# Buffers, queues and engines around the scores of a streamed recurrent attention kernel

## The chip, the cores and the metric

The kernel runs on one core of one Trainium2 chip. The core has a matrix engine (TensorE, PE in the profile, with its weight loads as PEld), a vector engine (VectorE, DVE), a scalar engine (ScalarE, ACT), GpSimd (POOL) and SyncE (SP), and 16 transfer engines that carry the DMAs of all queues. The metric is the device time of one launch in microseconds, the median of several runs. Each engine works through its own list of instructions in the order in which the kernel wrote them; semaphores hold an instruction back until what it needs is done.

## What is computed

Two blocks share a normalised input and are added to it. Block A is attention over segments of 32 rows that carry 8 rows of memory along; block B is a feed-forward block on the two rows that a router scores highest. Cut to what matters:

```python
x = A_x                                # 2048 x 1024, bf16
xn = layernorm(x)
# A: 64 segments in sequence, H = 32 heads of E = 128, M = 8 memory rows
for s in range(64):
    h = concat([mem, xn[32*s : 32*s+32]])          # 40 rows
    q, k, v = h @ Wq, h @ Wk, h @ Wv               # 1024 -> 32 x 128 each
    p = softmax(mask(q @ k.T * 128**-0.5))         # 40 x 40 for each head
    o = (p @ v) @ Wo                               # 4096 -> 1024
    mem, out[32*s : 32*s+32] = o[:8], o[8:]
# B: top 2 rows of xn @ w_r
y = (silu(xs @ w_gate) * (xs @ w_up)) @ w_down * sigmoid(r)
return x + out + xn + scatter(y)
```

The next segment's first 8 rows are this segment's result, so the segments run one after the other, each through all four weight matrices of 1024 x 4096.

## The kernel before

The weights of block A take 64 granules of 128 x 2048 bf16 (512 KB each): 48 for q, k and v, 16 for the output. 42 stay in SBUF (`wres`), 22 are fetched anew in every segment, evenly spread over the 64, into six slots (`wstream`, tile `g`). SyncE issues these fetches (L248): as soon as the matmuls of a granule have been written down, `used(g)` issues the fetch of the granule six places later into the same slot.

A prologue normalises x, writes its transposes to DRAM, computes block B's rows and folds them into the residual `zT_d`. Then come 64 segments, s = 4G + j. Each runs six phases, `PHASES`: q, k for heads 0 to 15 (half 0), q, k for half 1, then v for both halves. A phase is eight steps kc over the contraction. A step is four matmuls side by side, `PSm[32*jq...] += ST[:, kc] @ granule` (L502), where `ST` holds 24 rows of the segment and the 8 memory rows. After the phases come 16 steps w of the output projection into `WO` (L543), and the result goes through `mem_to_st` into the next segment's `ST` (L266, L267).

The 8 rows of a segment that don't fit into these 32 are called the left rows. They don't depend on the memory, so those of four segments are done together: at j = 1 and j = 2 the q and the k of the next group of four (phases with a second accumulator `PSl`, L506), at j = 0 the v of this group (phases 4 and 5), and at j = 3 their output projection (`WL`). Left q and k go through a transpose (`transposes_left`, L414) to DRAM, `qkl_d`, and come back for each segment and half as the tile `QKL` (`load_qkl`, L355).

Work of other kinds is hung into the phases by `hook(p, kc, fn)`, which runs fn after the matmuls of step kc of phase p:

- the transposes of q or k of a phase at step 1 of the next (`transposes`, into PSUM tile `PTq`, which VectorE copies to `QT` or `KT`), those of left rows at step 2;
- `fetch_z` at (1, 4): loads the residual `ZT` on ScalarE's queue, and has GpSimd copy its left rows to `ZL` and set them to zero (L394, L395);
- `scores(0)` at (2, 5) and `scores(1)` at (4, 5): GpSimd copies the left k from `QKL` behind the 32 others in `KT` (L428), TensorE makes the scores in PSUM (L432 to L437), VectorE and ScalarE the softmax (L442 to L461), and then the next `QKL` is loaded into the one buffer (L357, on ScalarE's queue): after half 0 that of half 1 of the same segment, after half 1 that of half 0 of the next;
- `attend(half, ph)`: two at (5, 2) and (5, 5), two between the steps of the projection. They need `VM[half]`, the v of that half, and `VL`. ScalarE copies the main rows of the result to `OT`, VectorE the left ones to `OTL` (L483, L485).

At the end of phases 4 and 5 the accumulator of v is copied to `VM`, the left columns 0 to 255 by ScalarE, the others by VectorE (L524, L525; L527 and L528 for `VL`). At the end of a segment ScalarE issues four stores of the result (L572) and at j = 3 four more of the left rows (L584).

All DMAs of SyncE and ScalarE take their semaphores in turn from one set of eight (DMAHW0 to DMAHW7 in the lists below), in the order in which the program wrote them down. A DMA that takes a semaphore waits until the one that had it eight places earlier has landed, and its queue waits with it.

PSUM has eight banks: two for `PSm` and `WO` (`psA`), one for `PSl` and `WL` (`psL`), two for transposes (`psT`), one for the scores, two for attend (`psO`).

Of the kernel before, what the change touches and what calls it, by code (L numbers as in the profile page):

```python
# [8 lines left out]
BF16 = mybir.dt.bfloat16  # L9
# [16 lines left out]
def kernel(  # L26
# [63 lines left out]
    psL = ctx.enter_context(tc.tile_pool(name="psL", bufs=1, space=PSUM))  # L90
    psT = ctx.enter_context(tc.tile_pool(name="psT", bufs=2, space=PSUM))
# [78 lines left out]
    def ln_c(t):  # L170

        TS[t] = []
        for src, what in ((XN[t], "x"), (xt(t), "z")):
            PTx = psT.tile([P, KC, 4, SEG], BF16, tag="t", name="PTx")
# [179 lines left out]
    def load_qkl(s, half):  # L354

        t = one.tile([P, 2, P], BF16, tag="qkl", name="QKL")
# [11 lines left out]
    QKL = None  # L368

    for s in range(NSEG):  # L370
# [14 lines left out]
        QT, KT, PTs, OT, nxt = {}, {}, {}, {}, {"qkl": QKL}  # L385
# [5 lines left out]
        def fetch_z():  # L391
            Zt = nxt["z"] = one.tile([P, KC, SEG], BF16, tag="zt", name="ZT")
            nc.scalar.dma_start(out=Zt[:, :, :], in_=zT_d[s])
            nc.gpsimd.tensor_copy(out=ZL[:, :, j, :], in_=Zt[:, :, XM:SEG])  # L394
# [30 lines left out]
        def scores(half):  # L425
            QKL = load_qkl(0, half) if s == 0 else nxt.pop("qkl")
# [14 lines left out]
            NM = two.tile([P, 8], F32, tag="nm", name="NM")  # L441
# [3 lines left out]
            DN = two.tile([P, 8], F32, tag="dn", name="DN")  # L445
# [17 lines left out]
            if s > 0 or half == 1:  # L463
                s1, half1 = (s, 1) if half == 0 else (s + 1, 0)
                if s1 < NSEG:
                    nxt["qkl"] = load_qkl(s1, half1)

        def attend(half, ph):
# [4 lines left out]
            for il in range(4):  # L473
                for jl in range(2):
# [10 lines left out]
            nc.vector.tensor_copy(out=OTL[:, h0:h0 + 8, j, :].rearrange("p (a i) r -> p a i r", a=2),  # L485
                                  in_=ov[:, :, :, SEG:NK])

        hook(1, 4, fetch_z)
        hook(2, 3, fetch_st)
        hook(2, 5, lambda: scores(0))  # L490
        hook(4, 5, lambda: scores(1))
        hook(5, 2, lambda: attend(0, 0))
        hook(5, 5, lambda: attend(0, 1))

        for p, (mat, half) in enumerate(PHASES):
# [16 lines left out]
            if mat < 2:  # L512
# [3 lines left out]
                if PSl is not None:  # L516
                    XBl = two.tile([P, 512], BF16, tag="xb", name="XBl")
                    nc.vector.tensor_copy(out=XBl[:, :], in_=PSl[:, :])  # L518
                    hooks.setdefault((p + 1, 2), []).insert(
                        0, lambda m=mat, h=half, b=XBl, g=left[mat]: transposes_left(m, h, b, g))  # L520
            else:
                c0 = half * 512
                VM[half] = one.tile([P, 512], BF16, tag="vm", name="VM")
                nc.scalar.copy(out=VM[half][:, 0:256], in_=PSm[:, 0:256])  # L524
                nc.vector.tensor_copy(out=VM[half][:, 256:512], in_=PSm[:, 256:512])  # L525
                if PSl is not None:
                    nc.scalar.copy(out=VL[:, c0:c0 + 256], in_=PSl[:, 0:256])  # L527
                    nc.vector.tensor_copy(out=VL[:, c0 + 256:c0 + 512], in_=PSl[:, 256:512])  # L528
# [42 lines left out]
        for g in range(4):  # L571
            nc.scalar.dma_start(out=out2[s * SEG:s * SEG + XM, 256 * g:256 * (g + 1)], in_=OB[32 * g:32 * g + XM, :])  # L572
# [6 lines left out]
        if j == 3:  # L579
            OL = one.tile([P, 256], BF16, tag="pm", name="OL")  # L580
            nc.scalar.copy(out=OL[:, :], in_=WL[:, 0:256])
            o4 = out2[4 * G * SEG:4 * (G + 1) * SEG, :].rearrange("(s r) d -> s r d", s=4)
            for g in range(4):
                nc.scalar.dma_start(out=o4[:, XM:SEG, 256 * g:256 * (g + 1)], in_=OL[32 * g:32 * (g + 1), :])  # L584
        if s + 1 < NSEG:
            ST, QKL = nxt["st"], nxt["qkl"]

# [34 lines left out]
```

## Time and profile before

| | |
|---|---|
| median of 3 runs | 2657.51 us (2650.09 to 2669.58) |
| the profiled execution | 2657.51 us, span 2655.6 us |
| mean granted TensorE clock | 0.862 |
| busy: PE, PEld, DVE, ACT, POOL | 1887.9, 981.6, 721.6, 465.0, 111.1 us |
| moved by DMA | 831.71 MB, mean 313 GB/s |
| of it the granules' queue (SyncE's) | 795.98 MB in 292148 packets |
| ScalarE's queue | 30.46 MB in 76352 packets |
| first segment, with block B ahead of it | 105.0 to 239.7 us |
| segments 1 to 62 | 239.7 to 2610.5 us |
| last segment and the end | 2610.5 to 2655.6 us |

In the profile a line like `POOL KT L428 <- DMA QKL<-qkl_d` names the engine, the tile that it writes and the line, and behind the arrow what ended its idle time. In lists of waits the numbers are the total in microseconds, how often, and the longest. An engine with a q behind its name (SPq, ACTq) is its sequencer, which issues the DMAs. The DMA share of a stretch is the mean busy share of the 16 transfer engines, counted from packets.

### The profile page before, as it was taken

Reading aid. Unit: us, or ns where it says so; the run is one execution under the profiler, and the core shown is the slowest. Engines: PE = TensorE matmul, PEld = TensorE weight load, DVE = VectorE, ACT = ScalarE, POOL = GpSimd, SP = SyncE. Lnnn points to the kernel's source line nnn. Section 1 sums busy time; section 2 is a strip of 40 time slices with the busy share of each in tenths; the row PEclk is TensorE's granted clock in tenths of the full one; section 3 lists DMA queues with packets and bytes.
Section 4 is the critical chain, followed back from the end, with each engine's and each line's share of the span. In section 5 each row is a group of like instructions: output and inputs, shape, how many; then the busy total and the mean of one; then the engine's idle time right before and its main releaser. Section 6 shows DMA issues by size and latency. Waiting matters only on the chain.

```text
span 2655.6 us, 82564 instructions
## 1 busy us (share of the span) xinstructions
PE 1887.9 (71%) x36873; PEld 981.6 (37%) x36873; DVE 721.6 (27%) x2021; ACT 465.0 (18%) x1017; POOL 111.1 (4%) x371
## 2 busy tenths in 40 slices
PE   4357777677777767776777777777777767777676
PEld 3223343334334333333434333333434333343333
DVE  5202223222222322222222322223232222223222
ACT  4201111111111111111111111111111111111111
POOL 4100000000000000000000000000000000000000
PEclk8578889988898889888988898788888888879888
DMA  9986989989898889989898988989899898989987
GB/s 350 325 316 214 346 299 330 322 301 330 297 333 306 311 308 317 327 301 336 311 327 308 326 307 314 324 297 328 306 321 323 309 321 291 343 280 336 327 289 273
DMA packets 368856, 831.71 MB, mean 313 GB/s; under 512 B 69458, under 2 KB 122738, under 8 KB 368500
## 3 DMA queue, kind: packets, MB, share of 16 engines
q1 hardware_dynamic: 292148, 795.98, 84.8%
q10 hardware_dynamic: 76352, 30.46, 4.2%
q8 instruction: 288, 4.72, 0.7%
q14 instruction: 68, 0.56, 0.1%
HBM read 804.28 MB, written 22.02 MB: 311 GB/s over the span
## 4 chain that ended last, share of the span: by engine, by line
DMA 47%; PE 26%; DVE 11%; issue 10%; ACT 2%; ACTq 1%; POOL 1%; SPq 1%; POOLq 0%; DVEq 0%
DMA QKL<-qkl_d 12%; DMA g<-in_A_Wk_dram 11%; PE PSm L502 9%; DMA g<-in_A_Wq_dram 9%; PE WO L543 7%; DMA out_dram<-OB 3%; DMA ZT<-zT_d 3%; DVE SPS L443 2%; DVE NM L442 2%; PE OP L478 2%; PE PSl L506 2%; DVE DN L446 1%; PE WL L543 1%; ACT SPS L444 1%; DMA xT_d<-Tx 1%
## 5 line engine op out<-in xcount | busy, mean ns | idle before, releaser
L502 PE MATMUL PSm<-wres,ST 128*32 128x512 bf16 x8192 | 813.1, 438 | 22.3 <-DVE ST L267 13.6
L502 PE MATMUL PSm<-g,ST 128*32 128x512 bf16 x4096 | 459.1, 433 | 153.9 <-DMA g<-in_A_Wq_dram 94.6
L502 PEld LDWEIGHTS <-ST 128*32 128x32 bf16 x12288 | 333.7, 103 | 583.8 <-issue 290.7
L506 PE MATMUL PSl<-wres,STL 128*32 128x512 bf16 x2048 | 226.5, 428 | 52.8 <-DVE VL L528 47.9
L514 ACT CAST XB<-PSm 128x512 bf16<-128x512 f32 x256 | 150.3, 587 | 632.6 <-PE PSm L502 457.0
L543 PE MATMUL WO<-wres,OT 128*32 128x256 bf16 x5120 | 238.7, 289 | 3.7 <-issue 3.7
L543 PEld LDWEIGHTS <-OT 128*32 128x32 bf16 x8192 | 220.2, 104 | 31.0 <-issue 10.1
L432 PE MATMUL SPS<-KT,QT 128*32 128x40 bf16 x2048 | 51.2, 188 | 191.2 <-POOL KT L428 191.2
L442 DVE TENSOR_REDUCE NM<-SPS 128x8 f32<-128x320 f32 x128 | 63.0, 492 | 451.0 <-PE SPS L437 451.0
L478 PE MATMUL OP<-PT,VM 32*128 32x40 bf16 x2048 | 102.3, 186 | 107.0 <-DVE VM L525 73.2
L543 PE MATMUL WO<-g,OT 128*32 128x256 bf16 x3072 | 171.8, 301 | 2.2 <-issue 1.5
L444 ACT ACTIVATE SPS<-SPS 128x320 f32<-128x320 f32 x128 | 54.1, 423 | 674.9 <-DVE SPS L443 558.2
L483 ACT CAST OT<-OP 128x256 bf16<-128x256 f32 x256 | 95.5, 373 | 430.2 <-PE OP L480 430.2
L404 PE MATMUL PTq<-IDENT,XB 128*128 128x128 bf16 x1024 | 110.7, 236 | 77.6 <-ACT XB L514 75.2
L485 DVE CAST OTL<-OP 128x64 bf16<-128x64 f32 x256 | 57.6, 225 | 353.0 <-ACT OT L483 353.0
L478 PEld LDWEIGHTS <-VM 32*128 32x128 bf16 x2048 | 70.2, 95 | 224.3 <-issue 83.7
L506 PEld LDWEIGHTS <-STL 128*32 128x32 bf16 x3072 | 92.4, 104 | 139.8 <-issue 89.6
L404 PEld LDWEIGHTS <-XB 128*128 128x128 bf16 x1024 | 63.2, 103 | 212.4 <-ACT XB L514 195.3
L412 DVE COPY KT<-PTq 128x512 bf16<-128x512 bf16 x128 | 54.4, 425 | 317.9 <-PE PTq L404 284.9
L409 DVE COPY QT<-PTq 128x512 bf16<-128x512 bf16 x128 | 52.4, 409 | 262.8 <-PE PTq L404 262.8
L434 PEld LDWEIGHTS <-QKL 128*8 128x8 bf16 x2048 | 38.4, 87 | 219.9 <-issue 112.7
L506 PE MATMUL PSl<-g,STL 128*32 128x512 bf16 x1024 | 109.7, 412 | 7.0 <-DVE XBl L518 7.0
(100 smaller groups left out, 1573.6 us busy)
## 6 DMA issues: line engine op xcount, KB each, us to landing
g<-in_A_Wq_dram SPq DMA_DIRECT2D x384, 512.0 KB
g<-in_A_Wo_dram SPq DMA_DIRECT2D x384, 512.0 KB
g<-in_A_Wk_dram SPq DMA_DIRECT2D x320, 512.0 KB
g<-in_A_Wv_dram SPq DMA_DIRECT2D x320, 512.0 KB
qkl_d<-QS ACTq DMA_DIRECT2D x64, 128.0 KB
QKL<-qkl_d ACTq DMA_DIRECT2D x128, 64.0 KB
g<-in_B_w_gate_dram SPq DMA_DIRECT2D x16, 448.0 KB
g<-in_B_w_up_dram SPq DMA_DIRECT2D x16, 448.0 KB
```

The costliest lines, as they stand in the source:

```text
L404: nc.tensor.transpose(out=PTq[:, il, :, :].rearrange("p j r -> p (j r)"), in_=XB[:, il * P:(il + 1) * P], identity=IDENT[:, :])
L412: nc.vector.tensor_copy(out=KT[half][:, :, 0:32], in_=pv)
L442: nc.vector.tensor_reduce(out=NM[:, :], in_=S8, axis=AX.X, op=ALU.max, negate=True)
L443: nc.vector.tensor_tensor(out=S8, in0=S8, in1=NM[:, :].unsqueeze(2).to_broadcast([P, 8, NK]), op=ALU.add)
L444: nc.scalar.activation(out=S8, in_=S8, func=ACTF.Exp, scale=SCALE)
L478: nc.tensor.matmul(o, lhsT=VM[half][q0:q0 + 32, il * P:(il + 1) * P], rhs=PTm[q0:q0 + 32, il, 0:NK], start=True, stop=False, tile_position ...
L483: nc.scalar.copy(out=OT[half][:, 2 * ph:2 * ph + 2, :, :], in_=ov[:, :, :, 0:SEG])
L485: nc.vector.tensor_copy(out=OTL[:, h0:h0 + 8, j, :].rearrange("p (a i) r -> p a i r", a=2), in_=ov[:, :, :, SEG:NK])
L502: nc.tensor.matmul(PSm[32 * jq:32 * jq + 32, :], lhsT=ST[:, kc, :], rhs=Gv[:, 512 * jq:512 * (jq + 1)], start=(kc == 0), stop=(kc == KC - ...
L506: nc.tensor.matmul(PSl[32 * jq:32 * jq + 32, :], lhsT=STL[:, kc, :], rhs=Gv[:, 512 * jq:512 * (jq + 1)], start=(kc == 0), stop=(kc == KC - 1),
L514: nc.scalar.copy(out=XB[:, :], in_=PSm[:, :])
L543: nc.tensor.matmul(PS[32 * g:32 * g + 32, 0:256], lhsT=lhs(h), rhs=Gv[:, D * hs + 256 * g:D * hs + 256 * (g + 1)], start=False, stop=(last ...
```

## The change

Five edits, with no change to the arithmetic:

- `QKL` gets two buffers. After scores(half) of segment s the left q and k of (s + 1, half) are loaded. Segment 0 loads its own at its scores, as before, and both of segment 1 at its end.
- `fetch_z` keeps only the load. GpSimd's copy to `ZL` and the memset become `split_z`, at (4, 6), behind scores(1).
- `VM` and `VL` are copied whole by ScalarE; so is `OTL` for half 0.
- `psL` gets two banks, `psT` one. In the prologue the transposes of z use `psO`. The transposes of left rows move from step 2 to step 3.
- The stores of a segment's result are put into a list `todo` and issued by SyncE in the next segment, at (0, 2), those of left rows at (0, 5). `NM` and `DN` go to one buffer each.

```diff
-    psL = ctx.enter_context(tc.tile_pool(name="psL", bufs=1, space=PSUM))
-    psT = ctx.enter_context(tc.tile_pool(name="psT", bufs=2, space=PSUM))
+    psL = ctx.enter_context(tc.tile_pool(name="psL", bufs=2, space=PSUM))
+    psT = ctx.enter_context(tc.tile_pool(name="psT", bufs=1, space=PSUM))
...
-        t = one.tile([P, 2, P], BF16, tag="qkl", name="QKL")
+        t = two.tile([P, 2, P], BF16, tag="qkl", name="QKL")
...
             nc.scalar.dma_start(out=Zt[:, :, :], in_=zT_d[s])
+
+        def split_z():
+            Zt = nxt["z"]
             nc.gpsimd.tensor_copy(out=ZL[:, :, j, :], in_=Zt[:, :, XM:SEG])
             nc.gpsimd.memset(Zt[:, :, XM:SEG], 0.0)
...
-            QKL = load_qkl(0, half) if s == 0 else nxt.pop("qkl")
+            QKL = load_qkl(0, half) if s == 0 else QKLs.pop(0)
...
-            if s > 0 or half == 1:
-                s1, half1 = (s, 1) if half == 0 else (s + 1, 0)
-                if s1 < NSEG:
-                    nxt["qkl"] = load_qkl(s1, half1)
+            if s == 0 and half == 1:
+                QKLs.append(load_qkl(1, 0))
+                QKLs.append(load_qkl(1, 1))
+            elif 0 < s < NSEG - 1:
+                QKLs.append(load_qkl(s + 1, half))
...
-            nc.vector.tensor_copy(out=OTL[:, h0:h0 + 8, j, :].rearrange("p (a i) r -> p a i r", a=2),
-                                  in_=ov[:, :, :, SEG:NK])
-
+            (nc.scalar.copy if half == 0 else nc.vector.tensor_copy)(
+                out=OTL[:, h0:h0 + 8, j, :].rearrange("p (a i) r -> p a i r", a=2), in_=ov[:, :, :, SEG:NK])
+
+        for n, fn in enumerate(todo):
+            hook(0, 2 + 3 * n, fn)
...
+        hook(4, 6, split_z)
...
-                    hooks.setdefault((p + 1, 2), []).insert(
+                    hooks.setdefault((p + 1, 3), []).insert(
...
-                nc.scalar.copy(out=VM[half][:, 0:256], in_=PSm[:, 0:256])
-                nc.vector.tensor_copy(out=VM[half][:, 256:512], in_=PSm[:, 256:512])
+                nc.scalar.copy(out=VM[half][:, :], in_=PSm[:, :])
                 if PSl is not None:
-                    nc.scalar.copy(out=VL[:, c0:c0 + 256], in_=PSl[:, 0:256])
-                    nc.vector.tensor_copy(out=VL[:, c0 + 256:c0 + 512], in_=PSl[:, 256:512])
+                    nc.scalar.copy(out=VL[:, c0:c0 + 512], in_=PSl[:, :])
...
-        for g in range(4):
-            nc.scalar.dma_start(out=out2[s * SEG:s * SEG + XM, 256 * g:256 * (g + 1)], in_=OB[32 * g:32 * g + XM, :])
+        def store(OB=OB, s=s):
+            for g in range(4):
+                nc.sync.dma_start(out=out2[s * SEG:s * SEG + XM, 256 * g:256 * (g + 1)],
+                                  in_=OB[32 * g:32 * g + XM, :])
+
+        todo = [store]
...
+                    nc.sync.dma_start(out=o4[:, XM:SEG, 256 * g:256 * (g + 1)], in_=OL[32 * g:32 * (g + 1), :])
+            todo.append(store_left)
```

What this makes of the order is seen at three places. First ScalarE's list where a group of four segments ends and the next begins (j = 3 to j = 0), before:

```order
L569 CAST OB<-WO 128x128 [waits DMAHW4_49,DMAHW6_49,DMAHW0_49,PE_49]
L572 DMA out_dram<-OB 24x256 [waits DMAHW2_49,DVE_49]
L572 DMA out_dram<-OB 24x256 [waits DMAHW3_49]
L572 DMA out_dram<-OB 24x256 [waits DMAHW4_49]
L572 DMA out_dram<-OB 24x256 [waits DMAHW6_49]
L581 CAST OL<-WL 128x256 [waits PE_49]
L584 DMA out_dram<-OL 4x8x256 [waits DMAHW0_49,Activation_49]
L584 DMA out_dram<-OL 4x8x256 [waits DMAHW1_49]
L584 DMA out_dram<-OL 4x8x256 [waits DMAHW3_49]
L584 DMA out_dram<-OL 4x8x256 [waits DMAHW4_49]
L514 CAST XB<-PSm 128x512 [waits PE_49]
```

The same place now:

```order
L575 CAST OB<-WO 128x128 [waits DMAHW4_49,DMAHW5_49,DMAHW3_49,PE_49]
L591 CAST OL<-WL 128x256 [waits DVE_49,PE_49]
L522 CAST XB<-PSm 128x512 [waits PE_49]
L394 DMA ZT<-zT_d 128x256 [waits DMAHW6_49,Pool_49]
L522 CAST XB<-PSm 128x512 [waits DVE_49,PE_49]
```

Eight stores stood ahead of the cast of the first phase's q (XB); now none does. They are in SyncE's list, among the granules of the next segment's phases:

```order
L248 DMA g<-in_A_Wq_dram 128x2048 [waits DMAHW1_49,PE_49]
L579 DMA out_dram<-OB 24x256 [waits DVE_49]
L579 DMA out_dram<-OB 24x256 [waits DMAHW2_49]
L579 DMA out_dram<-OB 24x256 [waits DMAHW3_49]
L579 DMA out_dram<-OB 24x256 [waits DMAHW5_49]
L248 DMA g<-in_A_Wq_dram 128x2048 [waits DMAHW6_49,PE_49]
L596 DMA out_dram<-OL 4x8x256 [waits DMAHW7_49,Activation_49]
L596 DMA out_dram<-OL 4x8x256 [waits DMAHW0_49]
L596 DMA out_dram<-OL 4x8x256 [waits DMAHW1_49]
L596 DMA out_dram<-OL 4x8x256 [waits DMAHW2_49]
L248 DMA g<-in_A_Wk_dram 128x2048 [waits DMAHW3_49,PE_49]
```

Before, SyncE's list had only granules there. Second, GpSimd's list of one segment, before:

```order
L394 COPY ZL<-ZT 128x8x8 [waits DMAHW7_49]
L395 MEMSET ZT 128x8x8 [waits PE_49,Pool_49]
L428 COPY KT<-QKL 128x16x8 [waits DVE_49,DMAHW1_49,PE_49,Activation_49]
L452 MEMSET PL 128x8x8 [waits DVE_49]
L428 COPY KT<-QKL 128x16x8 [waits DVE_49,DMAHW5_49,PE_49,Pool_49]
```

and now:

```order
L432 COPY KT<-QKL 128x16x8 [waits DVE_49,DMAHW2_49,PE_49,Activation_49]
L456 MEMSET PL 128x8x8 [waits DVE_49]
L432 COPY KT<-QKL 128x16x8 [waits DVE_49,DMAHW2_49,PE_49,Pool_49]
L398 COPY ZL<-ZT 128x8x8 [waits DMAHW5_49]
L399 MEMSET ZT 128x8x8 [waits Pool_49]
```

The two instructions on the residual moved from ahead of the first scores' copy to behind the second's. Third, VectorE's list from the end of the second softmax of a segment with j = 0 to the end of that segment's attention, before:

```order
L461 STREAM_TRANSPOSE PT_16609<-PL 128x256 [waits DVE_49]
L525 CAST VM<-PSm 128x256 [waits Activation_49]
L528 CAST VL<-PSl 128x256 [waits Activation_49]
L485 CAST OTL<-OP 128x8x8 [waits Activation_49] x2
L525 CAST VM<-PSm 128x256 [waits Activation_49]
L528 CAST VL<-PSl 128x256 [waits Activation_49]
L485 CAST OTL<-OP 128x8x8 [waits Activation_49] x2
```

and now:

```order
L465 STREAM_TRANSPOSE PT_16559<-PL 128x256 [waits DVE_49]
L490 CAST OTL<-OP 128x8x8 [waits Activation_49] x2
L576 CAST OB<-WO 128x128 [waits DMAHW2_49,DMAHW0_49,Activation_49]
```

The copies of v and the first pair of OTL left VectorE's list; ScalarE's has them.

More of the change, by code (lines that the diff above doesn't have):

```diff
@@ L367 @@
     STL = load_stl(0)
-    QKL = None
+    QKLs = []
+    todo = []
     for s in range(NSEG):
@@ L384 @@
             ZL = one.tile([P, KC, 4, XL], BF16, tag="zl", name="ZL")
-        QT, KT, PTs, OT, nxt = {}, {}, {}, {}, {"qkl": QKL}
+        QT, KT, PTs, OT, nxt = {}, {}, {}, {}, {}
         hooks = {}
@@ L440, in scores @@
             S8 = SPS.rearrange("p i a k -> p (i a) k")
-            NM = two.tile([P, 8], F32, tag="nm", name="NM")
+            NM = one.tile([P, 8], F32, tag="nm", name="NM")
             nc.vector.tensor_reduce(out=NM[:, :], in_=S8, axis=AX.X, op=ALU.max, negate=True)
@@ L444, in scores @@
             nc.scalar.activation(out=S8, in_=S8, func=ACTF.Exp, scale=SCALE)
-            DN = two.tile([P, 8], F32, tag="dn", name="DN")
+            DN = one.tile([P, 8], F32, tag="dn", name="DN")
             nc.vector.tensor_reduce(out=DN[:, :], in_=S8, axis=AX.X, op=ALU.add)
```

12 lines of the change are left out of this document (7 added, 5 removed).

## The prediction

> **What bounds the kernel now.** I read the profile's page first, then the busy time of stretches, the waits of TensorE, the chain of waits inside single segments, and the timeline where the chain pointed. The page first.
>
> ```profile
> span 2655.6 us, 82564 instructions
> ...
> DMA  9986989989898889989898988989899898989987
> ...
> DMA 47%; PE 26%; DVE 11%; issue 10%; ACT 2%; ACTq 1%; POOL 1%; SPq 1%; POOLq 0%; DVEq 0%
> DMA QKL<-qkl_d 12%; DMA g<-in_A_Wk_dram 11%; PE PSm L502 9%; DMA g<-in_A_Wq_dram 9%; PE WO L543 7%; DMA out_dram<-OB 3%; DMA ZT<-zT_d 3%; DVE SPS L443 2%; DVE NM L442 2%; PE OP L478 2%; PE PSl L506 2%; DVE DN L446 1%; PE WL L543 1%; ACT SPS L444 1%; DMA xT_d<-Tx 1%
> ```
>
> Two kinds of DMA share the chain: the weight granules g, and one small load, QKL, that takes 12% of it. The transfer engines are busy nine tenths of the time but not all of it. The next view is busy time by stretch: the loop without its first and last segment (62 segments), four neighbouring segments (s = 26, 28, 29, 31), and two short pieces in which TensorE was starved.
>
> ```profile
> core 0: us, PE busy (x) PEld busy (x) DVE busy (x) ACT busy (x) POOL busy (x), PEclk, DMA share, GB/s
> 239.70:2610.50 2370.80, 1738.74 (x34672) 890.33 (x34672) 641.81 (x1827) 402.45 (x911) 65.84 (x310) 0.88 0.91 316
> ...
> 1195.70:1233.40 37.70, 26.57 (x548) 13.93 (x548) 11.05 (x31) 6.87 (x15) 1.06 (x5) 0.95 0.94 328
> ...
> 1271.00:1308.20 37.20, 27.66 (x585) 14.22 (x576) 10.22 (x31) 6.62 (x16) 1.06 (x5) 0.91 0.85 297
> 1308.20:1346.20 38.00, 28.05 (x548) 14.06 (x548) 10.83 (x30) 6.87 (x15) 1.06 (x5) 0.91 0.94 330
> 1206.00:1222.00 16.00, 9.77 (x198) 4.58 (x197) 5.45 (x13) 2.54 (x5) 0.29 (x1) 1.00 1.01 364
> 1382.80:1416.90 34.10, 26.09 (x576) 14.07 (x580) 9.54 (x29) 5.70 (x13) 1.06 (x5) 0.90 0.98 345
> ...
> 1210.00:1214.00 4.00, 3.93 (x68) 1.98 (x72) 1.28 (x5) 0.00 (x0) 0.00 (x0) 1.00 1.04 405
> ```
>
> A segment takes 2370.8 / 62 = 38.2 us, with TensorE busy 1738.74 / 62 = 28.0. The DMA work of the loop is 0.91 x 2370.8 = 2157 us of 16 fully busy engines, 34.8 us a segment, and no part of the change takes a byte of it away. So 34.8 divided by the share that can be held is the floor of a segment. Shares above 1 occur because packets overlap. Now what stops TensorE in those 62 segments, and the queues behind it:
>
> ```profile
> PE SPS L432 <- POOL KT L428: 176.6, 67, 6.7
> PE PSm L502 <- DMA g<-in_A_Wq_dram: 91.6, 126, 3.6
> PE PTq L404 <- ACT XB L514: 74.3, 101, 3.8
> PE OP L478 <- DVE VM L525: 71.5, 47, 1.6
> PE PSl L506 <- DVE VL L528: 45.9, 15, 3.1
> PE PSm L502 <- DMA g<-in_A_Wk_dram: 38.1, 59, 2.3
> PE OP L478 <- ACT VM L524: 33.6, 36, 1.2
> ...
> PE PSm L502 <- DMA g<-in_A_Wv_dram: 15.2, 25, 1.8
> ...
> PE PTq L417 <- DVE XBl L518: 11.6, 15, 1.2
> ...
> POOL KT L428 <- DMA QKL<-qkl_d: 588.2, 57, 15.3
> ...
> SPq L248 <- DMA out_dram<-OB: 113.8, 44, 6.4
> ```
>
> Only 91.6 + 38.1 + 15.2 = 145 us of TensorE's idle time ends with a granule. The rest ends with a small dependence, and while TensorE stands at one the six granule slots fill up and the transfers stop: that is where the missing 9% of DMA share comes from. The change goes after these small dependences.
>
> **The change, part by part.** The cost of each is in TensorE's waits first; how much of that becomes time is settled at the end.
>
> Two QKL buffers. In segment 26 the load goes out when the first scores' exponential is running, lands 10.86 us later, and GpSimd's copy and the second scores hang on it:
>
> ```profile
> 1208.51 10.86 DMA QKL<-qkl_d
> ...
> 1219.52 0.30 POOL KT L428
> ```
>
> With two buffers the load for (s+1, half) is issued after scores(half) of s, a whole segment (38 us) ahead of its use. 10.86 us fits into that three times over, so this wait goes. It adds no transfer (two loads a segment as before) and its issue stays on ScalarE's queue in the same place.
>
> GpSimd's residual work later. It now stands ahead of the KT copy and waits for ZT:
>
> ```profile
> 1204.54 0.24 POOL L394 COPY ZL<-ZT 128x64 bf16<-128x64 bf16 x1 [26.51 <-DMA ZT<-zT_d]
> ...
> 1205.01 0.29 POOL L428 COPY KT<-QKL 128x128 bf16<-128x128 bf16 x1
> ```
>
> Placed behind both scores, it leaves the KT copy alone. Its own 0.24 us and the memset of ZT have phase 5, 8 kc steps, before the residual matmuls read them; I cost it at nothing. If that cover were short, the residual would wait under a microsecond. The two edits together take the 176.6 us. Between none of it (the load could be as late again) and all, I take all, since the lead is 38 us against 10.86.
>
> V copied by ScalarE. Now half of VM is VectorE's, and it stands behind the second softmax:
>
> ```profile
> 1222.22 0.37 ACT L524 CAST VM<-PSm 128x256 bf16<-128x256 f32 x1 [0.15 <-issue]
> ...
> 1222.65 0.19 PE L478 MATMUL OP<-PT,VM 32*128 32x40 bf16 x2 [0.97 <-ACT VM L524]
> ...
> 1224.02 0.39 DVE L525 CAST VM<-PSm 128x256 bf16<-128x256 f32 x1
> ...
> 1224.46 0.20 PE L478 MATMUL OP<-PT,VM 32*128 32x40 bf16 x2 [1.54 <-DVE VM L525]
> ```
>
> ScalarE copies 256 columns in 0.37 us and 512 (the XB rows below) in 0.59. The whole of VM would have been ready at 1222.22 + 0.59 = 1222.8 instead of 1224.4; attend's first matmuls wait 0.97 us for ScalarE there already and 1.54 more for VectorE. So the 71.5 us go, and the 33.6 us stay and grow by 62 x 0.22 = 14. Gain 71.5 - 14 = 57 us. ScalarE also takes OTL of half 0, 64 columns: an estimate from the two durations is 0.37 - 0.75 x 0.22 = 0.21 us, twice a segment. With VM (2 x 0.22) that is 0.86 us a segment on an engine busy 402.45 of 2370.8 us; what it can delay is VM of half 1, which has the residual and four projections ahead of its use. Bounds: 0 to 0.86 us a segment lost, I take 0.
>
> Two PSUM banks for left rows. PSl of phase 5 no longer waits until VectorE has emptied that of phase 4: 45.9 us in the loop goes, whole. The bank is taken from the transposes. Those of left rows move from kc 2 to kc 3, which removes most of the 11.6 us for XBl, but now need VectorE's copy of the previous transpose out of the one bank. In phase 3 this copy stands behind the first softmax, and in the rows above VectorE came free of a softmax at 1224.02, 4.2 us after the KT copy that ended at 1219.82. A gain is excluded, since a bank less frees nothing; the loss is at most 4.2 us in one phase of the 16 segments with j = 1, 67 us. I take 12, which cancels the 11.6: nearer the low end, since TensorE has two kc steps with left rows, the next phase's first two and the transposes themselves to do in those 4.2 us.
>
> Outputs issued by SyncE. Now ScalarE issues 4 stores a segment and 4 more each fourth, and at those boundaries the cast of XB is behind them:
>
> ```profile
> 1272.66 3.04 ACTq L584 DMA_DIRECT2D out_dram<-OL  x4
> 1275.74 0.59 ACT L514 CAST XB<-PSm 128x512 bf16<-128x512 f32 x1 [3.11 <-DMA out_dram<-OL]
> ...
> 1276.38 0.51 PE L404 MATMUL PTq<-IDENT,XB 128*128 128x128 bf16 x4 [2.02 <-ACT XB L514]
> ```
>
> TensorE loses 2.02 us there; 15 such boundaries give 30 of the 74.3. The stores now stand in SyncE's queue between granules. By the order, each DMA waits for the one eight places earlier, so the fourth store is past when three granules are still in flight, and the next fetch needs a slot that is only free later than that. Issuing four took 3.04 us in the row above with its waits, under the time of those three granules (22 a segment, 34.8 / 22 = 1.6 us each). I cost it at nothing; SyncE's wait for store landings exists already (113.8 us). The OL buffer shares its place with PM, so at j = 0 VectorE's PM now waits until the later store of OL has landed; it has two phases for that.
>
> The sum. Removed in the loop: 176.6 + 57 + 45.9 + 30 = 310 us, which leaves 2061, 145 of it granule waits. That is under the DMA work of 2157. So DMA decides, and granule waits grow by what the others shrink beyond it. The share that it holds is the number to choose: 0.94 in segments 26 and 29, 0.98 in the shortest of the rows, segment 31, 1.01 over 16 us of starving. TensorE keeps some short waits but has time to spare, so I take 0.99, between the last two and nearest the whole segment: 2157 / 0.99 = 2179, a gain of 192. Outside the loop, the first and the last segment:
>
> ```profile
> PE PSl L506 <- DVE XBl L518: 9.2, 4, 3.7
> ...
> PE PSl L506 <- DVE VL L528: 2.1, 1, 2.1
> ...
> PE SPS L432 <- POOL KT L428: 3.7, 1, 3.7
> ...
> PE OP L478 <- DVE VM L525: 1.7, 1, 1.7
> ```
>
> 9.2 + 2.1 + 3.7 + 1.7 = 16 us. The profiled execution took 2657.51 us (span 2655.6), which is also the median. 2657.5 - 192 - 16 = 2450 us.
>
> The stretches of 405 and 364 GB/s can be set against a page: the Trainium skill, "DMA: Bandwidth & Descriptors", section "Where 436 GB/s comes from", puts what HBM gives one core at about 358 GB/s. By that, as an estimate, the loop's 316 x 2370.8 bytes need at least 2093 us and the kernel 2364. The measured rows are above it, so it is no ceiling for short stretches here.
>
> **The rivals.** (A) The slots never fill, and DMA runs at the 1.04 of the 4 us row: 2157 / 1.04 = 2074, gain 297 + 16, 2345 us. For it: TensorE's remaining 2061 less granule waits is far under. Against: no whole segment has passed 0.98. (B) New short waits, the one transpose bank and the loaded ScalarE, take the place of those removed, some 3 us a segment; the slots fill as before and the share stays at the 0.94 of segments 26 and 29: 2157 / 0.94 = 2295, gain 76 + 16, 2566 us. (C) Slower: SyncE's queue is blocked by the stores. One landing took
>
> ```profile
> 1270.06 5.00 DMA out_dram<-OB
> ```
>
> and if each of four waited for the one before it, 20 us a segment stand ahead of the granules. Six slots cover 6 x 38.2 / 22 = 10.4 us, 9.6 stay: 62 x 9.6 - 208 = +387, 3045 us. It decides from 10.4 + 208 / 62 = 13.8 us of blocking. Against: lanes reach eight back, not one. (D) The change doesn't pay: 0.91 is all that this mix of transfers holds, every removed wait comes back as a granule wait, and only the 16 us outside are won: 2641. Against: 0.98 and 1.01 in rows above.
>
> Gating could also move TensorE's side: the granted clock in the loop is 0.88. The Trainium skill, "TensorE: Matmul & The Clock Gate", Part 1, says that idle stretches of some 3.4 us drop the clock to half and sustained work restores it. By that, as an estimate, fewer long waits would give back up to 12% of TensorE's busy time, which speaks against B. The clocks of the single segments above, 0.90 to 0.95, can't settle it.
>
> **How the numbers follow.** Forecast 0.68, A 0.10, B 0.14, D 0.05, C 0.03. The forecast's own bounds are shares of 1.02 (2115, so 2386) and 0.95 (2271, so 2542). The range 2380 to 2570 takes these and most of B, and leaves out some 0.2. One per cent, 26.6 us, is about what a measurement of this kernel can tell from no change (its runs spread over 19.5). Faster by more: forecast, A and B, 0.92; within: D, 0.05; slower: C, 0.03.
>
> **What would show it.** Right: the wait of KT for QKL gone from GpSimd and KT from TensorE's list, apart from the first segment; DVE VM and VL gone; granule waits risen from 145 to some 260 us (2179 - 1739 busy, less the 632 - 145 - 310 of other idle time); DMA share of the loop at 0.97 or more, and the segments with j = 0 no longer the poorest at 0.85. Wrong: a share still under 0.95, with PTq waiting for VectorE's copies (B), or SyncE waiting more than 10 us a segment for stores (C). A clock that falls would show a TensorE that has become the bound.

## The result, and the profile after

| | before | after |
|---|---|---|
| median, 4 runs each | 2662.41 us | 2568.62 us (2564.14 to 2575.26) |
| ratio, 95% interval | | 0.9654 [0.9608, 0.9701] |
| profiled execution, span | 2657.51, 2655.6 us | 2564.14, 2562.2 us |
| segments 1 to 62 | 2370.8 us | 2285.3 us |
| TensorE waits for granules, whole run | 150 us | 405 us |

The kernel became 94 us faster, where 207 were forecast. Of the profiled executions, the loop of 62 segments gives 85.5 of the 93.4 us and what lies around it 7.9.

The page after, three lines of it: the span, the DMA share in 40 slices, and the chain by engine and by line.

```profile
span 2562.2 us, 82489 instructions
...
DMA  9997999999999989989998999999998998999898
...
DMA 62%; PE 27%; issue 4%; DVE 3%; ACT 2%; SPq 2%; ACTq 1%; POOL 0%; DVEq 0%; POOLq 0%
DMA g<-in_A_Wv_dram 15%; DMA g<-in_A_Wq_dram 14%; DMA g<-in_A_Wo_dram 13%; PE PSm L510 12%; DMA g<-in_A_Wk_dram 6%; PE WO L549 4%; PE PSl L514 3%; DMA qkl_d<-QS 2%; DMA QKL<-qkl_d 2%; PE WL L549 2%; DMA ZT<-zT_d 2%; PE PTq L408 1%; DMA ST<-xT_d 1%; SPq L248 1%; DMA zT_d<-Tz 1%
```

QKL fell from 12% of the chain to 2%; granules now carry 48%. SyncE's sequencer, SPq, shows 2%: a small number that matters below. Next, the loop of the kernel after, in the view of stretches, columns as in the prediction.

```profile
core 0: us, PE busy (x) PEld busy (x) DVE busy (x) ACT busy (x) POOL busy (x), PEclk, DMA share, GB/s
235.57:2520.82 2285.25, 1721.77 (x34672) 884.74 (x34672) 561.18 (x1548) 449.35 (x1035) 62.67 (x310) 0.90 0.93 328
```

The DMA share rose from 0.91 to 0.93 only; the forecast needed 0.99. The waits of TensorE in the kernel after, whole run (us in total, times, longest):

```profile
PE PSm L510 <- DMA g<-in_A_Wk_dram: 136.0, 93, 5.7
PE PSm L510 <- DMA g<-in_A_Wq_dram: 99.9, 109, 4.1
PE PSm L510 <- DMA g<-in_A_Wv_dram: 85.2, 111, 3.7
PE WO L549 <- DMA g<-in_A_Wo_dram: 83.8, 152, 2.3
...
PE PTq L408 <- ACT XB L522: 33.6, 84, 1.3
...
PE OP L483 <- ACT VM L532: 14.4, 28, 1.3
...
PE SPS L436 <- POOL KT L432: 10.7, 2, 6.6
PE PTq L421 <- DVE QT L413: 10.6, 11, 1.3
```

Every wait that the change went after is gone or small, and 405 us of granule waits stand in their place. So TensorE waits for transfers while the transfer engines idle 7% of the time. What holds the transfers back must stand ahead of them, in the queue that issues them. SyncE's own waits in the kernel after:

```profile
SPq L248 <- PE PSm L510: 311.7, 364, 6.2
SPq L248 <- DMA qkl_d<-QS: 174.6, 48, 8.8
...
SPq L248 <- DMA QKL<-qkl_d: 136.7, 60, 5.1
...
SPq L579 <- DMA g<-in_A_Wk_dram: 66.3, 61, 3.5
...
SPq L248 <- DMA ZT<-zT_d: 57.2, 26, 3.5
...
SPq L596 <- DMA g<-in_A_Wq_dram: 18.1, 15, 2.3
...
SPq L596 <- DMA ZT<-zT_d: 10.6, 7, 3.6
SPq L579 <- DMA g<-in_A_Wq_dram: 10.6, 19, 1.1
```

L248 are granule fetches, L579 and L596 the stores. In the first row a fetch waits for TensorE to free a slot; the rows with qkl_d, QKL and ZT are waits for transfers that ScalarE issued. The stores wait 66.3 + 18.1 + 10.6 + 10.6 = 106 us for their semaphores, with every fetch behind them standing still. Their issue itself, in the views of the two lines (minimum, median and maximum in ns):

```profile
L579 SPq DMA_DIRECT2D out_dram<-OB x256: 302/352/1460, 237.1 to 2556.8; - x128
```
```profile
L596 SPq DMA_DIRECT2D out_dram<-OL x64: 615/618/773, 352.2 to 2559.3; - x64
```

256 x 0.352 + 64 x 0.618 = 130 us. With the 106 that is 236 us, 3.7 us a segment, in which SyncE can't fetch, whether or not a slot is free. One place shows what that does, the start of segment 28, where a group of four begins. SyncE's timeline (start, us, what):

```profile
1239.80 0.33 SPq L248 DMA_DIRECT2D g<-in_A_Wq_dram  x1
1240.18 1.61 SPq L579 DMA_DIRECT2D out_dram<-OB  x4
1241.89 0.36 SPq L248 DMA_DIRECT2D g<-in_A_Wq_dram  x1
1244.02 2.65 SPq L596 DMA_DIRECT2D out_dram<-OL  x4
1246.78 1.67 SPq L248 DMA_DIRECT2D g<-in_A_Wk_dram  x3
```

The same microseconds in stretches of two:

```profile
1240.00:1242.00 2.00, 1.74 (x32) 0.76 (x24) 0.00 (x0) 0.59 (x1) 0.00 (x0) 1.00 0.54 156
1242.00:1244.00 2.00, 1.98 (x35) 0.76 (x32) 0.42 (x1) 0.40 (x1) 0.00 (x0) 1.00 0.92 295
1244.00:1246.00 2.00, 1.16 (x16) 0.55 (x17) 0.43 (x1) 0.19 (x1) 0.00 (x0) 1.00 0.53 183
1246.00:1248.00 2.00, 0.56 (x21) 0.32 (x24) 0.00 (x0) 0.00 (x0) 0.00 (x0) 0.73 0.19 59
```

And the end of the chain of waits there:

```profile
1244.20 0.47 SPq L596
...
1246.06 0.62 SPq L596
...
1246.78 4.57 DMA g<-in_A_Wk_dram
```

From 1240.18 to 1246.78 SyncE issues eight stores and one granule. The first store of the left rows waits 1.7 us, until 1244.02, for the landing of the granule issued at 1239.80. In the program's order that granule stands eight places ahead of it: behind it come ScalarE's loads of ZT and ST, the four stores of OB and one more granule. So when the left rows' stores begin, a single granule is still in flight, the one of 1241.89. (In seven cases it is ScalarE's ZT that a store of left rows waits for, 10.6 us in all.) Three fetches go out together at 1246.78, so SyncE reached them after their slots had come free; the DMA share has fallen to 0.19 by then.

### The profile page after: what moved, and what is told of

It is laid out like the page before. It is cut to its first block, busy times and chain, and to the rows that moved or that the text cites. A ratio compares the mean times of both kernels' runs of the same rounds, so it can differ in the third digit from the quotient of the medians.

```text
span 2562.2 us, 82489 instructions
## 1 busy us (share of the span) xinstructions
PE 1865.3 (73%) x36873; PEld 975.1 (38%) x36873; DVE 638.4 (25%) x1733; ACT 513.5 (20%) x1145; POOL 108.0 (4%) x371
## 3 DMA queue, kind: packets, MB, share of 16 engines
q10 hardware_dynamic: 64832, 26.25, 3.8%
## 4 chain that ended last, share of the span: by engine, by line
DMA 62%; PE 27%; issue 4%; DVE 3%; ACT 2%; SPq 2%; ACTq 1%; POOL 0%; DVEq 0%; POOLq 0%
DMA g<-in_A_Wv_dram 15%; DMA g<-in_A_Wq_dram 14%; DMA g<-in_A_Wo_dram 13%; PE PSm L510 12%; DMA g<-in_A_Wk_dram 6%; PE WO L549 4%; PE PSl L514 3%; DMA qkl_d<-QS 2%; DMA QKL<-qkl_d 2%; PE WL L549 2%; DMA ZT<-zT_d 2%; PE PTq L408 1%; DMA ST<-xT_d 1%; SPq L248 1%; DMA zT_d<-Tz 1%
## 5 line engine op out<-in xcount | busy, mean ns | idle before, releaser
L510 PE MATMUL PSm<-wres,ST 128*32 128x512 bf16 x8192 | 785.2, 423 | 15.7 <-DVE ST L267 13.6
L510 PE MATMUL PSm<-g,ST 128*32 128x512 bf16 x4096 | 450.9, 427 | 325.8 <-DMA g<-in_A_Wk_dram 136.0
L549 PE MATMUL WO<-wres,OT 128*32 128x256 bf16 x5120 | 248.2, 293 | 17.3 <-issue 17.3
L514 PE MATMUL PSl<-wres,STL 128*32 128x512 bf16 x2048 | 210.4, 398 | 2.7 <-DMA STL<-stl_d 2.7
L408 PE MATMUL PTq<-IDENT,XB 128*128 128x128 bf16 x1024 | 112.9, 240 | 35.6 <-ACT XB L522 33.6
L432 POOL COPY KT<-QKL 128x128 bf16<-128x128 bf16 x128 | 37.3, 291 | 2335.4 <-PE WO L549 1057.4
L490 DVE CAST OTL<-OP 128x64 bf16<-128x64 f32 x128 | 28.8, 225 | 406.8 <-ACT OT L488 406.8
L514 PEld LDWEIGHTS <-STL 128*32 128x32 bf16 x3072 | 86.3, 100 | 70.8 <-issue 14.0
L483 PE MATMUL OP<-PT,VM 32*128 32x40 bf16 x2048 | 94.9, 180 | 19.3 <-ACT VM L532 14.4
L485 PE MATMUL OP<-PT,VL 32*128 32x40 bf16 x2048 | 88.1, 176 | 4.2 <-ACT VL L534 4.2
```

The source lines that it names most:

```text
L408: nc.tensor.transpose(out=PTq[:, il, :, :].rearrange("p j r -> p (j r)"), in_=XB[:, il * P:(il + 1) * P], identity=IDENT[:, :])
L483: nc.tensor.matmul(o, lhsT=VM[half][q0:q0 + 32, il * P:(il + 1) * P], rhs=PTm[q0:q0 + 32, il, 0:NK], start=True, stop=False, tile_position ...
L485: nc.tensor.matmul(o, lhsT=VL[q0:q0 + 32, c0:c0 + P], rhs=PTl[q0:q0 + 32, il, 0:NK], start=False, stop=True, tile_position=(q0, 0), skip_g ...
L510: nc.tensor.matmul(PSm[32 * jq:32 * jq + 32, :], lhsT=ST[:, kc, :], rhs=Gv[:, 512 * jq:512 * (jq + 1)], start=(kc == 0), stop=(kc == KC - ...
L514: nc.tensor.matmul(PSl[32 * jq:32 * jq + 32, :], lhsT=STL[:, kc, :], rhs=Gv[:, 512 * jq:512 * (jq + 1)], start=(kc == 0), stop=(kc == KC - 1),
L549: nc.tensor.matmul(PS[32 * g:32 * g + 32, 0:256], lhsT=lhs(h), rhs=Gv[:, D * hs + 256 * g:D * hs + 256 * (g + 1)], start=False, stop=(last ...
```

## The experiments

Two readings stood against each other. Theory 1: the stores in SyncE's queue hold the granules back, by their own issue time and by the eight semaphores that SyncE and ScalarE take in turn. Theory 2: the engines can't hold more than some 0.93 in this mix. A third was the prediction's rival B: the one transpose bank and the loaded ScalarE make new waits.

**Stores elsewhere.** From the kernel after, the stores issued by ScalarE at the end of the segment, as before (e1); or left at their new place but issued by GpSimd, whose DMAs take semaphores of their own (e2).

```diff
-                nc.sync.dma_start(out=out2[s * SEG:s * SEG + XM, 256 * g:256 * (g + 1)],
+                nc.gpsimd.dma_start(out=out2[s * SEG:s * SEG + XM, 256 * g:256 * (g + 1)],
...
-                    nc.sync.dma_start(out=o4[:, XM:SEG, 256 * g:256 * (g + 1)], in_=OL[32 * g:32 * (g + 1), :])
+                    nc.gpsimd.dma_start(out=o4[:, XM:SEG, 256 * g:256 * (g + 1)], in_=OL[32 * g:32 * (g + 1), :])
```

> The changed kernel, but with the stores issued by ScalarE at the end of the segment, as before the change. Theory 1 (SyncE's queue: the eight stores issued there take the queue's time and hold the granule fetches, so the transfer engines run dry): faster than the changed kernel's 2568 us, 2480 to 2530, though ScalarE's cast waits behind its stores again at the group boundary; DMA share of the loop over 0.94. Theory 2 (the transfer engines carry no more than a share of 0.93 of this mix, any wait removed comes back): 2568 within 13. Theory 3 (one transpose bank and ScalarE's added copies cost what the rest won): 2570 to 2600, ScalarE's load is the same and its stores are added.

> The changed kernel with the stores at their new place but issued by GpSimd, whose DMAs have semaphores of their own, so that they hold neither SyncE's nor ScalarE's queue. Theory 1: 2500 us or less, DMA share 0.96 or more, and the granule wait for Wk at the start of groups (136 us in all) under 60. Theories 2 and 3: 2568 within 13.

Measured: e1 2480.41 us, 0.9351 [0.9310, 0.9393]; e2 2374.88 us, 0.8932 [0.8894, 0.8971]. The loop of e2:

```profile
231.93:2347.74 2115.81, 1637.71 (x34672) 865.37 (x34672) 558.44 (x1548) 448.25 (x1035) 225.43 (x619) 0.95 0.98 354
```

Who issues 320 small stores is worth 2568.6 - 2374.9 = 194 us, and the share is 0.98. Theory 2 falls.

**One edit alone.** The kernel before with two QKL buffers and the residual work moved; `NM` and `DN` have one buffer each, as in the change, and nothing else is different.

```diff
-        t = one.tile([P, 2, P], BF16, tag="qkl", name="QKL")
+        t = two.tile([P, 2, P], BF16, tag="qkl", name="QKL")
...
+        hook(4, 6, split_z)
```

> The kernel before with only the two QKL buffers and GpSimd's residual work behind the scores. Theory 1: 2590 to 2620, since the waits for v and XB stay and fill the slots. Theory 2: the share rises to 0.93 here already, 2570 to 2590. Theory 3: as fast as the changed kernel or faster, 2530 to 2570, since the costs of the other edits are missing.

Measured: 2483.90 us, 0.9357 [0.9316, 0.9399]. A miss: the edit alone brings 170 us, more than the whole change, and as much as the change without its new store place (e1, 2480). So the copies of v and the banks together bring nothing that e1 shows, and the stores on SyncE take back 85 to 88. Yet the waits that those two edits remove still stand in e3's list for TensorE:

```profile
PE OP L482 <- DVE VM L530: 67.9, 48, 1.6
...
PE PSl L511 <- DVE VL L533: 47.9, 16, 3.1
```

In e1 these 116 us are gone, and its granule waits stand at 309 us against 193. That reads as: a wait removed from TensorE pays only if SyncE has issued the next granules by then.

**More stores and fewer.** From the kernel after: each store cut in two by columns (e5, 640 stores of the same bytes); and only the first of four stores of each group (e6; three quarters of the output's columns aren't written, except in the last segment and the last group).

```diff
-                nc.sync.dma_start(out=out2[s * SEG:s * SEG + XM, 256 * g:256 * (g + 1)],
-                                  in_=OB[32 * g:32 * g + XM, :])
+                for c in range(2):
+                    c0 = 256 * g + P * c
+                    nc.sync.dma_start(out=out2[s * SEG:s * SEG + XM, c0:c0 + P],
+                                      in_=OB[32 * g:32 * g + XM, P * c:P * (c + 1)])
```
```diff
-            for g in range(4):
+            for g in range(4 if s == NSEG - 1 else 1):
...
-                for g in range(4):
+                for g in range(4 if G == NT - 1 else 1):
```

> The changed kernel with each store on SyncE's queue cut into two of half the columns: the same bytes and places, 640 stores in place of 320. Theory 1 (each store on that queue costs granule time, by its issue and its turn at a shared semaphore): the changed kernel is 194 us above the one with the stores on GpSimd, 0.6 us a store, so about 2760, and at least 2650. Rival (it is the place of the stores or their bytes, not their number): 2570 to 2610.

> The changed kernel with one store of the four of each group left out but the first, for all segments and groups except the last; three quarters of the output columns of those rows are not written. Theory 1 by the same 0.6 us a store: 2375 + 50, 2400 to 2450. Rival (the cost is that SyncE has to wait for a store at all): 2500 to 2568.

Measured: e5 2693.94 us, 1.0138 [1.0072, 1.0204], 1.4% slower than the kernel before, though less slow than the 2760 expected; e6 2406.83 us, 0.9083 [0.9007, 0.9158]. The left-out stores of e6 are 3 of the 832 MB. With e2 the series is complete: 0 stores on SyncE 2375, 86 stores 2407, 320 stores 2569, 640 stores 2694. Rival C's mechanism is there; with twice the stores even its sign would have come true.

**What of a store costs: its issue, or the shared semaphores?** e4 is e2 with every small transfer of ScalarE (loads of ZT, ST, STL and QKL, stores to qkl_d) issued by GpSimd too. SyncE's granules then share semaphores with nobody. e13 is e4 with the result's stores back on SyncE.

```diff
-        nc.scalar.dma_start(out=ST.rearrange("p k r -> p (k r)"), in_=xT_d[s // 4][s % 4])
+        nc.gpsimd.dma_start(out=ST.rearrange("p k r -> p (k r)"), in_=xT_d[s // 4][s % 4])
...
-        nc.scalar.dma_start(out=t[:, :, :], in_=qkl_d[s // 4][:, half, :, s % 4, :].rearrange("m p c -> p m c"))
+        nc.gpsimd.dma_start(out=t[:, :, :], in_=qkl_d[s // 4][:, half, :, s % 4, :].rearrange("m p c -> p m c"))
...
-            nc.scalar.dma_start(out=Zt[:, :, :], in_=zT_d[s])
+            nc.gpsimd.dma_start(out=Zt[:, :, :], in_=zT_d[s])
```

> As the second of these, and the small loads and stores of the loop (ZT, ST, STL, QKL, the left q and k) issued by GpSimd as well, so that SyncE's granule fetches share their eight semaphores with no other DMA. Theory 1, if the shared semaphores take a part beside the stores' issue: another 20 to 60 us under the second, 2440 to 2480; if the stores' issue is all of it: as the second. Theory 2: 2568 within 13. GpSimd makes its descriptors in software, so that its own queue could become late: then KT waits show on TensorE.

> As e4_small_pool (GpSimd issues ZT, ST, STL, QKL and the qkl_d stores), but the result's stores stand in SyncE's queue as in the changed kernel. SyncE's list then holds granules and stores alone, and each waits only for what SyncE itself issued eight places earlier. Two readings of the 194 us between the changed kernel and e2_stores_pool: (a) the stores take SyncE's own time, 4 to 8 issues in a row at 0.4 to 0.6 us each, whatever semaphore they wait on: then the gap to e4's 2309 stays at 150 to 200, 2460 to 2510 us. (b) it is the semaphores that the stores and granules take in turn with ScalarE's small transfers, so that a fetch waits for a landing of another queue: then most of the gap goes, 2310 to 2370 us. In between, both count, and the split is read from the time.

| | small transfers on ScalarE (shared) | on GpSimd |
|---|---|---|
| stores on SyncE | 2568.62 (after) | 2393.76 (e13), 0.9041 [0.9002, 0.9080] |
| stores on GpSimd | 2374.88 (e2) | 2309.40 (e4), 0.8686 [0.8628, 0.8744] |

Both count, and they make each other worse. e13 lies between the two bands that were set for it, and e4 gains slightly more over e2 than the 20 to 60 us expected. With semaphores of their own the stores cost 84 us, within the 130 us of SyncE's time that their issue takes. The small transfers on ScalarE cost 65 us without the stores and 175 with them. Of the 259 us between the corners, 109 belong to the pair. The loops of e13 and e4:

```profile
229.35:2354.18 2124.83, 1633.96 (x34672) 854.15 (x34672) 559.00 (x1549) 438.11 (x1035) 264.73 (x635) 0.95 0.98 353
```
```profile
232.03:2271.16 2039.13, 1597.33 (x34672) 844.17 (x34672) 558.42 (x1549) 438.11 (x1035) 428.77 (x941) 0.96 1.00 368
```

e4 is the fastest of all, 13% under the kernel before. With the small transfers on GpSimd, every wait of SyncE's list for QKL, qkl_d, ZT or ST is gone: 389 us in the kernel after and 461 in e2, none in e13 and e4. Their sum isn't their price, since more of them in e2 cost less. Nor does the move change the semaphores alone. It loads GpSimd (428.77 us busy in the loop against 225.43 in e2). It takes waits out of ScalarE's own list: TensorE's wait for XB is 84.6 us in e2 and 56.0 in e4. And the small transfers go in fewer packets (11776 in e13 against 64832 in the kernel after, for the same 26 MB): their share of the transfer engines falls from 3.8% of 2562 us to 3.0% of 2393, so that packets account for some 25 of the 175 us, and by the same sum for some 22 of the 65. The rest fits the semaphores, but no run separates them from ScalarE's list. What stops TensorE most in e4 is again a small one:

```profile
PE SPS L436 <- POOL KT L432: 61.0, 33, 7.3
```

**The store edit alone.** The kernel before with only the stores moved to SyncE, at the places of the kernel after.

```diff
-        for g in range(4):
-            nc.scalar.dma_start(out=out2[s * SEG:s * SEG + XM, 256 * g:256 * (g + 1)], in_=OB[32 * g:32 * g + XM, :])
+        def store(OB=OB, s=s):
+            for g in range(4):
+                nc.sync.dma_start(out=out2[s * SEG:s * SEG + XM, 256 * g:256 * (g + 1)],
+                                  in_=OB[32 * g:32 * g + XM, :])
+
+        todo = [store]
```

> The kernel before with one edit: the stores issued by SyncE in the next segment, at the places of the changed kernel. If the stores cost SyncE's queue the same here as in the changed kernel (85 us against the QKL edit alone, 2484 to 2569), the time is 2650 + 85 less up to 30 for the XB casts that no longer wait, 2700 to 2740 us. If the slots that stand full while TensorE waits for KT cover the queue, so that the stores cost only once the other waits are gone, it is 2620 to 2670, no change.

Measured: 2653.67 us, 1.0008 [0.9980, 1.0036], no change. The time would fit stores that are covered there, but TensorE's waits tell otherwise. Those of the kernel before, whole run, and below them those of e14:

```profile
PE SPS L432 <- POOL KT L428: 191.2, 70, 6.7
PE PSm L502 <- DMA g<-in_A_Wq_dram: 94.6, 128, 3.6
PE PTq L404 <- ACT XB L514: 75.2, 103, 3.8
...
PE PSm L502 <- DMA g<-in_A_Wk_dram: 38.9, 60, 2.3
```
```profile
PE PSm L505 <- DMA g<-in_A_Wk_dram: 130.3, 104, 5.3
PE PSm L505 <- DMA g<-in_A_Wq_dram: 119.7, 135, 4.4
PE SPS L433 <- POOL KT L429: 76.9, 64, 5.8
...
PE PTq L405 <- ACT XB L517: 33.0, 79, 2.1
```

With this edit the wait for KT falls by 114 us and that for XB by 42; the granule waits of Wq and Wk rise by 116. With those of Wv and Wo it is 301 us against 150, so 151 up for 156 down. Waits that merely change places inside one stretch would look the same, but the stretches differ. From a segment's first scores to its second (starts of the mask's matmul, mean of segments 1 to 62) the time grows from 10.3 to 11.6 us, and from there to the next segment's first scores it falls from 28.0 to 26.7. So the edit has a gain and a price of like size. That fits its price beside the two QKL buffers: they take the KT waits away by themselves, so most of the gain has nothing left to act on.

**The banks and v.** e7: e2 with the copies of v and OTL divided between ScalarE and VectorE as before. e8: e2 with the old banks and the left transposes at step 2. e9: the same on e4. e10: e2 with step 2 alone. e11: the kernel after with the old banks and step 2. e12: e9 with the load of the next ST issued behind the first scores, one load less ahead of GpSimd's copy into KT; 10 to 30 us under e9 were expected.

```diff
-                nc.scalar.copy(out=VM[half][:, :], in_=PSm[:, :])
+                nc.scalar.copy(out=VM[half][:, 0:256], in_=PSm[:, 0:256])
+                nc.vector.tensor_copy(out=VM[half][:, 256:512], in_=PSm[:, 256:512])
```
```diff
-    psL = ctx.enter_context(tc.tile_pool(name="psL", bufs=2, space=PSUM))
-    psT = ctx.enter_context(tc.tile_pool(name="psT", bufs=1, space=PSUM))
+    psL = ctx.enter_context(tc.tile_pool(name="psL", bufs=1, space=PSUM))
+    psT = ctx.enter_context(tc.tile_pool(name="psT", bufs=2, space=PSUM))
...
-                    hooks.setdefault((p + 1, 3), []).insert(
+                    hooks.setdefault((p + 1, 2), []).insert(
```

> The kernel with the stores on GpSimd, but v and the left rows of the attention copied as before the change, half by VectorE. If ScalarE's copies are worth what their wait measured (57 us by the prediction), 2410 to 2440. If the wait hangs on TensorE at a time when the transfer engines have work anyway, within 15 of 2375, as the step from the QKL edit alone to the change with ScalarE's stores suggests (2484 to 2480).

> The kernel with the stores on GpSimd, but the PSUM banks as before the change (one for left rows, two for transposes, left transposes at step 2). If the second bank is worth the wait for VL (46 us) 2400 to 2425; if the single transpose bank costs as much as it, 2375 within 12; if theory 3 holds, faster than 2363.

> The kernel with all small DMAs on GpSimd, with the PSUM banks and the step of the left transposes as before the change. The banks and the step together cost 48 us where granules share semaphores with the small loads (2375 against 2327). If that is the bank itself (TensorE held by the single transpose bank), the same step is seen here: 2255 to 2275. If it is the order (the left transposes' store, one step later, takes its turn at the semaphores in another place among the granules), it is gone where nothing is shared: 2309 within 15.

> The kernel with the stores on GpSimd and the changed banks, but the left transposes at step 2 as before the change. If the bank is the cost: 2370 to 2400, the single bank waits more at step 2. If the step (the order of the DMAs) is the cost: near 2327, 2315 to 2345.

> The changed kernel itself (stores on SyncE) with the PSUM banks and the step of the left transposes as before. If the 48 us are there as well, 2510 to 2530; if SyncE's stores hide them, 2568 within 15.

| | us | ratio, interval | against |
|---|---|---|---|
| e7 | 2388.43 | 0.8998 [0.8941, 0.9054] | e2, 0.8932: 14 us slower, intervals overlap |
| e8 | 2327.02 | 0.8770 [0.8712, 0.8828] | e2: 48 us faster |
| e9 | 2328.76 | 0.8783 [0.8721, 0.8845] | e4, 0.8686: no gain |
| e10 | 2371.10 | 0.8936 [0.8890, 0.8982] | e2: the same |
| e11 | 2566.76 | 0.9666 [0.9611, 0.9722] | after, 0.9654: the same |
| e12 | 2315.20 | 0.8745 [0.8702, 0.8787] | e9: 14 us faster, intervals overlap |

In the change itself the banks are worth nothing (e11), and v divided again is no faster (e7), so rival B's mechanism doesn't explain 2569. The 48 us between e2 and e8 need the old banks, since the step alone does nothing (e10), and they are gone once the granules share no semaphore (e9). SyncE's waits for ScalarE's transfers are 415 us in e8 against 461 in e2 and 490 in e10. That speaks for another turn of the semaphores rather than for a bank as such, but the old banks with step 3 weren't run, and this cause stays open. In e12 the wait for KT is 43.2 us against 53.5 in e9; whether the time gained by it can't be told.

## Why the prediction was right or wrong

- **QKL and GpSimd's work: right, and its price too.** The 176.6 us of KT waits left the loop; the 10.7 us that remain are in segment 0. Alone the edit brought 170 us (e3).
- **V by ScalarE: the wait went, the time hardly.** DVE VM is off the list and ACT VM fell to 14.4 us, where 48 were expected. The term of 57 us was worth some 14 (e7 against e2, intervals overlap), and together with the banks 4 in e1 against e3.
- **Two banks for left rows: the wait went, the time not.** The 45.9 us were worth nothing (e11), and with the stores on GpSimd the old banks were even the faster ones (e8). As a wait, the loss by one transpose bank was sized right: 10.6 us for QT and 3.0 for KT against 12.
- **XB behind ScalarE's stores:** 74.3 fell to 33.6, somewhat more than the 30 taken.
- **Stores on SyncE: the step that failed.** The prediction had: "Issuing four took 3.04 us in the row above with its waits, under the time of those three granules", and so "I cost it at nothing". They took 236 us of SyncE's time. Against their old place on ScalarE they cost 88 us (e1), where the prediction had a gain of 30 from the XB waits; against GpSimd they cost 194 (e2). With the stores left where they were the change brings 174 us (e1), near the 207. The prediction let the fourth store pass with three granules still in flight; it left out that ScalarE's loads take places in the same count, and at 1244 us above one granule was in flight. The sentence asked whether the queue gets past the stores before the last granule in flight lands. It should have asked whether a freed slot is refilled at once: in a loop bound by transfers, a fetch issued late lets the engines run low even while another is in flight, as at 1246 us above with a share of 0.19. It also checked only that a store waits eight places back, and not that the granule behind takes part in the same turn with ScalarE's small transfers.
- **The share of 0.99: right as a limit, not reached for that reason.** With the queue free the loop holds 0.98 (e2) and 1.00 (e4). The 0.93 after is neither what the engines can do (rival D) nor what short waits leave (B).
- **Rival B gave 2566 and the time was 2569, but not by its mechanism:** the waits for VectorE's transposes are small, and the old banks change nothing. That the time lies at the upper end of the range, inside it, is luck: no term of the forecast leads there. It was rival C's mechanism at a smaller price. C put 20 us of blocking on a segment and asked 13.8 to decide; there were 3.7, and they cost from the first stores on (86 of them 32 us, e6 against e2). The cover of six slots that C allowed isn't there when slots have just come free, as at 1246 us above.
- **DMA work of 2157 us, "no part of the change takes a byte of it away": the bytes stayed, the work didn't.** Share times length of the loop is 0.93 x 2285 = 2125 after, 2073 in e2 and 2039 in e4, for the same 749 to 750 MB (316 x 2371 and 368 x 2039). The floor was some 5% too high, which is how e4 came under rival A's 2345. This error made the forecast too slow, and so hid part of what the stores cost.
- **Outside the loop:** 7.9 us for 16 (the four rows of the prediction add up to 16.7).

The 2364 us that the prediction set beside its sum, from the figure of about 358 GB/s in the Trainium skill, "DMA: Bandwidth & Descriptors", "Where 436 GB/s comes from", isn't a floor here: e4 moved 368 GB/s over 2039 us and ran 2309 us. The same page of the Trainium skill says under "Issuing engines are not separate DMA queues" that starting DMAs on several engines saves only the sequencer's time, usually small beside the transfer. Here it wasn't small: the stores' issue takes 130 us of SyncE's time, and the stores cost 84 us where nothing else is shared (e13 against e4). More goes with the other 175 of the 259 us between e4 and the kernel after, those of the small transfers on ScalarE, which the sequencer's time doesn't explain.

## What to carry to other kernels

When transfers decide, give the queue that fetches the stream nothing else to do, and let it share semaphores with no other queue; price each foreign instruction there at its issue time plus its wait, with nothing for cover: here that gave 236 us, an upper bound to the 194 lost. The value of a removed wait isn't a sum: here 170 (QKL alone) and 0 (stores alone) made 94 together with the rest, so edits are best run alone first. A time that comes out as a rival said doesn't confirm the rival's mechanism; the waits do.

## What was unexpected of the hardware

- A store takes longer to issue on GpSimd, 0.51 us in the mean against a median of 0.352 on SyncE, and yet the kernel is 194 us faster with the stores there: here it counted whose queue they stood in. The line of e2, busy us and mean ns:

```profile
L579 POOL DMA_DIRECT2D out_dram<-OB x256 | 129.1, 511 | 1373.8 <-DVE OB L576 1344.6 <-issue 29.2
```

- The same bytes took less DMA busy time the less the queue stalled, 2157 us before and 2039 in e4. e4 also moved them in fewer packets (314583 for the run against 368856 before), but e2 didn't (367576) and still came to 2073, so packets aren't all of it. The rest is open.
- The granted TensorE clock rose together with the share, 0.88 in the loop before, 0.90 after, 0.96 in e4, and TensorE's busy time for the same 34672 matmuls fell from 1739 to 1597 us.
